# First loads reordered, the product with g split around the first scores, and one turn a step later in a chunked-attention-plus-MLP kernel

## The chip, the cores and the metric

The kernel runs on one core of a Trainium2 chip. The number that counts is device time in microseconds (us), and lower is better. Before the change the median of 7 runs is 225.18 us, the lowest 224.84 and the highest 226.16. Besides these there is one profiled execution, whose records are shown below.

## The reference

Two stages follow each other. The first is attention in chunks of 32 queries. Each chunk sees 16 keys to the left of it, its own 32, 8 to the right, and 8 memory keys. The second is a normalisation without bias, a product with `w_ch1`, a relu, a product with `w_ch2`, and a residual.

```python
# q, k, v: (4, 8, 768, 64); mem_k, mem_v: (4, 8, 8, 64)
for c in range(24):
    l, r = max(0, 32 * c - 16), min(768, 32 * c + 40)
    k_full = concat(mem_k, k[:, :, l:r]); v_full = concat(mem_v, v[:, :, l:r])
    a = softmax(q[:, :, 32 * c : 32 * c + 32] @ k_full.T / 8)
    attn[:, :, 32 * c : 32 * c + 32] = a @ v_full
x = attn with heads side by side                     # (4, 768, 512)
xn = (x - mean(x)) / sqrt(var(x) + 1e-6) * g_ln
out = x + relu(xn @ w_ch1) @ w_ch2                   # 512 -> 2048 -> 512
```

## The kernel before, in words

The tokens of the four batches are cut into 24 tiles of 128, six to a batch. Three tiles make a unit of 384 tokens, so there are eight units. The order of all work is written out by hand, because each engine executes its own list in order. A tile's attention consists of these steps:

- `scores(b, t)` (L303): 16 matmuls of keys against queries, 64 contraction rows each. They read the key windows `KT` and the queries `QR`, both with the head dimension on partitions.
- `soften` (L313): two exponentials on ScalarE.
- `values` (L324): 16 matmuls against `V`. Then VectorE divides by the sum of the exponentials (reciprocal L331, product L332) and forms the mean.
- `norm` (L344, VectorE): subtracts the mean and multiplies by `gb`, which is g spread over 128 partitions.
- `turn_x` (L372 and L377): transposes the normalised tile `xn` to `xT`. For tiles in `ON_PE` it uses four TensorE transposes and a VectorE copy; for others it uses a DMA transpose. `stats` and `root` form the standard deviation beside this, on ScalarE and GpSimd.

A unit's MLP is `up` (L398, 4 matmuls of 384 columns and a relu) sixteen times, then `down` (L424, 4 matmuls of 512 columns) twelve times. For unit 0 the first pieces are done tile by tile in `up_tile` (L409, 16 matmuls of 128 columns), because its tiles are finished one at a time.

Keys and queries must be turned so that the head dimension lies on partitions. A block of 256 tokens is rearranged by VectorE (`mix`, L104), turned by eight TensorE transposes (`transpose_block`, L218) and copied to the key windows (`window`, `pieces`) or to `QR` (`part_q`, `whole_q`). The first block of batch 0 comes in float32 over the queues of SyncE (SP) and ScalarE (ACT) into `raws`, and is narrowed by `mix_raw`. Its queries come in two halves of 64 partitions, lower and upper, with an even and an odd part each. `first_q` turns one half, and `first_copy` copies it to `QR`. All else is loaded by GpSimd (POOL), narrowing from float32 to float16 on the way: `load_block` (L120), `load_v` (L128), `load_w1` (L140) and `load_w2` (L145). GpSimd's list alternates loads with memsets, and at most eight loads are in flight, each on its own semaphore.

`mem_keys` turns the memory keys and `memT` copies them to `memKT`; `mem_cols` puts them into the last 8 columns of each window. `v_mem` copies memory values into the last 8 rows of `V`. `warm` (L462) issues matmuls of zeros, whose result nobody reads. PSUM slots come from rings: two `att` slots and four `mm` slots, taken in turn by `slot`.

After the opening (L552 to L629) a plan is followed: units 0 to 7 with 28 steps each. In steps 0 to 15 of a unit one `up` goes first, in steps 16 to 27 one `down` (unit 0 is already past most of its `up`s and begins at step 12). Then come the pieces that `at(u, step, fn, ...)` has put there. `attend(8, 12, 16, 1)` is the attention of the last tile of unit 2, which is done during unit 1; its `turn_x` is at step 19. Batch 1's first loads, `early` (memsets of its `V` and `KT` on GpSimd) and `mem_v_loads` are at steps 14 and 15 of unit 0.

Of the kernel before, what the change touches and what calls it, by code (L numbers as in the profile page):

```python
# [8 lines left out]
FP32 = mybir.dt.float32  # L9
# [6 lines left out]
def kernel(  # L16
# [32 lines left out]
    memkf = sb.tile([128, 2, 64], FP32, name="memkf")  # L49
    memk16 = sb.tile([128, 2, 64], FP16, name="memk16")  # L50
# [49 lines left out]
    def copy(eng, out, in_):  # L100
        if eng is nc.scalar:
            eng.copy(out=out, in_=in_)
        else:
            eng.tensor_copy(out=out, in_=in_)  # L104
# [45 lines left out]
    def mem_keys():  # L150
        p = slot("att")
        pv = as16(p[:, 0, :])
        for half in range(2):
            for par in range(2):
                nc.tensor.matmul(
                    out=pv[64 * par : 64 * par + 64, 128 * half : 128 * half + 128],
                    lhsT=memk16[:, half, :], rhs=identity,
                    is_transpose=True, start=True, stop=True, tile_position=(0, 64 * par),
                )
        mem_slot.append(pv)  # L160
# [3 lines left out]
    def memT():  # L164
        pv = mem_slot[0]
        for par in range(2):
            rows = slice(64 * par, 64 * par + 64)
            nc.vector.tensor_copy(
                out=memKT[rows, :, :, :].rearrange("p b j m -> p b (j m)"),
                in_=free(pv[rows, :], 32 * par, [[64, 4], [1, 32]]),  # L170
            )
# [88 lines left out]
    def first_q(half, pvs):  # L260

        i = pick(iv, ("b", 0, 0, 1))
        rows = slice(64 * half, 64 * half + 64)
        for r in range(8):
            pv, c = (pvs[r // 4], 128 * (r % 4)) if len(pvs) == 2 else (pvs[0], 128 * r)
            nc.tensor.matmul(
                out=pv[:, c + 64 * half : c + 64 * half + 64],
                lhsT=i[rows, 128 * r : 128 * r + 128], rhs=identity[rows, rows],
                is_transpose=True, start=True, stop=True, tile_position=(64 * half, 0),
            )  # L270

    def first_copy(half, pvs):

        n = 8 // len(pvs)
        for m, pv in enumerate(pvs):
            copy((dve, act)[m], free(QR[0], 512 * m + 64 * half, [[128, n], [1, 64]]),
                 free(pv, 64 * half, [[128, n], [1, 64]]))
# [188 lines left out]
    nc.scalar.dma_start(out=grow, in_=dram(moe_g_ln, 0, [[512, 1], [1, 512]]))  # L466
# [9 lines left out]
    nc.sync.dma_start(out=memkf, in_=dram(mem_k, 0, [[64, 128], [128 * 64, 2], [1, 64]]))  # L476
    first_load(1, 0, 0, 16, nc.sync)
    first_load(1, 1, 0, 16, nc.scalar)

    def load_mem_v(b, eng):  # L480
        eng.dma_start(
            out=xs[5 + b][96:W, :], in_=dram(mem_v, b * 4096, [[64, 8], [512, 8], [1, 64]])
        )

    load_mem_v(0, nc.sync)
    first_load(1, 0, 16, 32, nc.sync)
    first_load(1, 1, 16, 32, nc.scalar)
# [18 lines left out]
    def mem_vals(b):  # L506
        copy(act, memv16[96:W, b, :, 0:64], xs[5 + b][96:W, :].rearrange("p (h d) -> p h d", h=8))

    make_identity(nc, identity)
    load_block(0, 1, 0)  # L510
    nc.gpsimd.memset(V[0].bitcast(FP32)[0:32, 0, :, :], 0.0)
    ones(0, 0, 2, pool)
    nc.vector.memset(zero, 0.0)
# [34 lines left out]
    load_v(0, 11)  # L548
    load_w2(2)
# [4 lines left out]
    warm(4)  # L554
    p = slot("att")
    nc.tensor.matmul(out=p[:, 0, :], lhsT=gone, rhs=grow, start=True, stop=True)
    mix_raw(0, raws[0], 0, dve)
    mix_raw(0, raws[0], 1, act)
    copy(dve, memk16, memkf)
    copy(act, gb, p[:, 0, :])  # L560
    warm(1, 128)
    transpose_block(0, 0, 0, K0)
    mem_keys()
    warm(1, 512, mm[2])
    window(0, 0, K0, 0, dve)
    mix_raw(1, raws[1], 0, dve, 0, 64)
    mix_raw(1, raws[1], 1, act, 0, 64)
    first_q(0, Q0)
    memT()
    window(0, 0, K0, 1, act)  # L570
    mem_cols(0, dve)
    first_copy(0, Q0)
    warm(1, 512, p[:, 1, :])
    scores(0, 0)
    mem_vals(0)
# [3 lines left out]
    rest = [as16(att[0][:, 0, :])]  # L579
    first_q(1, rest)  # L580
    v_mem(0, 0, 2, dve)
    first_copy(1, rest)
    warm(1, 512, mm[2])
    mix(0, 1, 0, dve)
    values(0, 0)
# [7 lines left out]
    warm(2, 512, p[:, 1, :])  # L593
# [4 lines left out]
    turn_x(0, 0)  # L598
# [36 lines left out]
    def attend(i, s0, s1, u):  # L635

        b, t = divmod(i, NT)
        at(u, s0, scores, b, t)
        at(u, s0, soften, b, t, 0)
        at(u, s0 + 1, soften, b, t, 1)  # L640
        at(u, s1, values, b, t)
        at(u, s1 + 1, norm, b, t)
        at(u, s1 + (3 if i in ON_PE else 2), turn_x, b, t)
        at(u, s1 + 2, stats, b, t)
        if i < 6:
            at(1, i % 3, root, b, t)
        else:
            at(i // 3 - 1, (20, 22, 23)[i % 3], root, b, t)

    def early(b):  # L650
        ones(1, 0, NG, pool)
        nc.gpsimd.memset(V[1][0:32, 0, :, :], 0.0)
        nc.gpsimd.memset(V[1][64:96, NG - 1, :, :], 0.0)
        clear_keys(1, pool)

    def mem_v_loads(b):
        for i in range(1, B):
            load_mem_v(i, nc.gpsimd)
# [14 lines left out]
    for b in range(1, B):  # L673
        at(0, 22 + b, mem_vals, b)
# [12 lines left out]
    order[1:1] = [(mem_v_loads, ()), (early, ())] + [(root0, (t,)) for t in range(3)]  # L687
    for n, (fn, args) in enumerate(order):
        at(0, 14 + n // 2, fn, *((1,) + args))
# [101 lines left out]
```

## Time and profile before

| | |
|---|---|
| median of 7 runs (lowest, highest) | 225.18 us (224.84, 226.16) |
| the profiled execution's own time | 224.52 us |
| its span | 222.8 us |
| TensorE busy | 213.7 us (96%) |
| weight loads busy | 131.2 us (59%) |
| VectorE, ScalarE, GpSimd busy | 134.3, 103.9, 98.9 us |
| moved by DMA | 27.72 MB, 124 GB/s on average |

The span is the time from the first to the last instruction, and 1.7 us of the execution lie around it. Busy time is the union of an engine's instructions. A matmul's record includes the time until its result is through, so a TensorE row can be busy while matmuls issue slowly. In a timeline row the first number is the start, the second the duration, and the bracket at the end says how long the engine sat idle ahead of it and what ended that.

### The profile page before, as it was taken

How to read it: one execution, taken by the hardware profiler on the slowest of the kernel's cores; microseconds unless marked ns; L12 is line 12 of the kernel's file. 1: busy time of each engine (PE TensorE's matmuls, PEld its weight loads, DVE VectorE, ACT ScalarE, POOL GpSimd, SP SyncE). 2: the span in 40 equal slices, each digit the busy share in tenths (PEclk: the TensorE clock that was granted, in tenths of full speed). 3: DMA queues.
4: the chain of work that ended last, by engine and by line, in shares of the span. 5: the costliest groups of instructions: out<-in, count | busy, mean ns of one | idle time of the engine just before them, and what ended most of it. 6: DMA issues, size and time to landing. Idle time of an engine off the chain costs nothing.

```text
span 222.8 us, 4976 instructions
## 1 busy us (share of the span) xinstructions
PE 213.7 (96%) x1957; PEld 131.2 (59%) x1957; DVE 134.3 (60%) x330; ACT 103.9 (47%) x220; POOL 98.9 (44%) x172
## 2 busy tenths in 40 slices
PE   7789999999998999999999999999999999999994
PEld 1457986557664566546664567446654666456553
DVE  6675586687869658834675678716845367234221
ACT  3472558547783146733781067424851365103200
POOL 8667653899888896211923793300021011100000
PEclk9999999999999999999999999999999999999999
DMA  6999999799999999898995799494112201211012
GB/s 145 204 196 191 201 192 205 135 64 212 191 102 146 229 183 146 93 160 197 130 158 99 99 159 169 74 205 115 21 30 74 94 14 36 71 55 42 0 47 94
DMA packets 72225, 27.72 MB, mean 124 GB/s; under 512 B 60273, under 2 KB 68209, under 8 KB 72202
## 3 DMA queue, kind: packets, MB, share of 16 engines
q0 software_dynamic: 45728, 14.61, 61.8%
q1 hardware_dynamic: 26168, 12.28, 25.9%
q10 hardware_dynamic: 306, 0.53, 0.8%
q8 instruction: 15, 0.25, 0.5%
q14 instruction: 8, 0.07, 0.1%
HBM read 30.28 MB, written 6.29 MB: 164 GB/s over the span
## 4 chain that ended last, share of the span: by engine, by line
PE 70%; DMA 19%; POOL 6%; DVE 3%; issue 1%; DVEq 0%; POOLq 0%
PE mm L398 31%; PE mm L424 30%; DMA w2c<-in_moe_w_ch_dram 8%; DMA w1c<-in_moe_w_ch_dram 4%; PE att L303 4%; DMA V<-in_v_dram 3%; DMA st<-in_q_dram 3%; PE att L324 3%; PE mm L446 2%; POOL V L128 1%; POOL st L120 1%; POOL rstd L359 1%; DVE xs L332 1%; POOL veps L355 0%; DVE V L104 0%
## 5 line engine op out<-in xcount | busy, mean ns | idle before, releaser
L424 PE MATMUL mm<-w2c,rT 128*128 128x512 f16 x368 | 82.8, 379 | 0.0
L398 PE MATMUL mm<-xT,w1c 128*128 128x384 f16 x448 | 78.6, 327 | 0.2 <-DVE KT L104 0.2
L398 PEld LDWEIGHTS <-w1c 128*128 128x128 f16 x448 | 49.1, 114 | 22.4 <-issue 0.4
L424 PEld LDWEIGHTS <-rT 128*128 128x128 f16 x368 | 34.9, 98 | 39.7
L392 DVE TENSOR_SCALAR rT<-mm 128x384 f16<-128x384 f32 (+1 forms) x61 | 34.3, 567 | 25.3 <-PE mm L398 21.9
L390 ACT ACTIVATE rT<-mm 128x384 f16<-128x384 f32 (+1 forms) x63 | 31.4, 502 | 38.2 <-PE mm L398 20.9
L313 ACT ACTIVATE AT<-att,band 104x512 f16<-104x512 f32 x48 | 31.3, 685 | 28.3 <-PE att L303 28.3
L128 POOL DMA_DIRECT2D V<-in_v_dram x48 | 38.3, 810 | 4.1 <-DMA w1c<-in_moe_w_ch_dram 2.7
L433 DVE SCALAR_TENSOR_TENSOR osb<-mm,rstd,xs 128x512 f32<-128x512 f32 x23 | 17.2, 749 | 34.2 <-PE mm L424 29.6
L355 POOL TENSOR_SCALAR veps<-sq 128x1 f32<-128x1 f32 x24 | 7.3, 303 | 62.0 <-ACT junk L349 48.3
L349 ACT ACTIVATE junk<-xs,nmean 128x512 f16<-128x512 f32 x24 | 17.3, 722 | 15.0 <-DVE nmean L338 13.1
L344 DVE SCALAR_TENSOR_TENSOR xn<-xs,nmean,gb 128x512 f16<-128x512 f32 x24 | 17.9, 747 | 0.4
L332 DVE SCALAR_TENSOR_TENSOR xs<-att,rec 128x512 f32<-128x512 f32 x24 | 16.6, 692 | 0.8
L303 PE MATMUL att<-QR,KT 64*104 64x64 f16 x384 | 16.0, 235 | 0.1
L303 PEld LDWEIGHTS <-KT 64*104 64x104 f16 x384 | 12.7, 135 | 4.8 <-issue 2.5
L359 POOL TENSOR_TENSOR rstd<-veps,mhalf 128x1 f32<-128x1 f32 x24 | 14.4, 598 | 2.0
L120 POOL DMA_DIRECT2D st<-in_q_dram x22 | 12.7, 593 | 5.0 <-DMA w2c<-in_moe_w_ch_dram 2.0
L409 PE MATMUL mm<-xT,w1c 128*128 128x128 f16 x192 | 13.8, 235 | 0.5 <-DVE xT L377 0.5
L120 POOL DMA_DIRECT2D st<-in_k_dram x22 | 13.2, 620 | 2.0 <-DVE xT L377 1.6
L409 PEld LDWEIGHTS <-w1c 128*128 128x128 f16 x192 | 12.7, 119 | 1.1 <-issue 1.0
L324 PEld LDWEIGHTS <-AT 104*64 104x64 f16 x384 | 8.4, 114 | 8.1 <-issue 3.9
L331 DVE RECIPROCAL rec<-att 128x8 f32<-128x8 f32 x24 | 4.9, 206 | 13.3 <-PE att L324 12.9
(79 smaller groups left out, 148.1 us busy)
## 6 DMA issues: line engine op xcount, KB each, us to landing
out_dram<-osb SPq DMA_DIRECT2D x23, 256.0 KB, 2.2
V<-in_v_dram POOLq DMA_DIRECT2D x40, 96.0 KB, 5.7
st<-in_k_dram POOLq DMA_DIRECT2D x22, 128.0 KB, 5.6
st<-in_q_dram POOLq DMA_DIRECT2D x22, 128.0 KB, 6.8
w1c<-in_moe_w_ch_dram POOLq DMA_DIRECT2D x4, 512.0 KB, 9.7
w2c<-in_moe_w_ch_dram POOLq DMA_DIRECT2D x4, 512.0 KB, 8.8
V<-in_v_dram POOLq DMA_DIRECT2D x8, 80.0 KB, 5.4
xT<-xn SPq DMA_TRANSPOSE x17, 2.8
```

Of the source, the lines that this page charges most:

```text
L120: nc.gpsimd.dma_start(out=s[:, 512 * par : 512 * par + 512], in_=dram((k, q)[which], (b * H + 4 * par) * HS + blk * 256 * D, [[512, 32], [ ...
L128: nc.gpsimd.dma_start(out=V[b % 2][lo:hi, g, :, 0:64], in_=dram(v, b * H * HS + (64 * g - 16 + lo) * D, [[64, hi - lo], [HS, H], [1, 64]]),)
L303: nc.tensor.matmul(out=p[0:W, par, (4 * gg + j) * 64 : (4 * gg + j) * 64 + 64], lhsT=KT[b % 2][rows, 2 * t + gg, j, :], rhs=free(QR[b % 2] ...
L313: nc.scalar.activation(out=free(AT[t % 3], 32 * c, [[64, 16], [1, 32]]), in_=free(p, 4 * c, [[64, 16], [1, 4], [8, 8]], W), func=ACTF.Exp, ...
L332: nc.vector.scalar_tensor_tensor(out=x.rearrange("p (h d) -> p h d", h=8), in0=free(p, 0, [[128, 8], [1, 64]]), scalar=1.0, in1=free(r, 0, ...
L344: nc.vector.scalar_tensor_tensor(out=xn[i % 4], in0=xs[i % 9], scalar=nmean[t], in1=gb, op0=ALU.add, op1=ALU.mult,)
L349: nc.scalar.activation(out=junk, in_=xs[(NT * b + t) % 9], func=ACTF.Square, bias=nmean[t], scale=1.0, accum_out=sq[t],)
L390: nc.scalar.activation(out=o, in_=p, func=ACTF.Relu)
L392: nc.vector.tensor_scalar(out=o, in0=p, scalar1=0.0, scalar2=None, op0=ALU.max)
L398: nc.tensor.matmul(out=p, lhsT=free(w1c[c][:, dt, :], i, [[4, 128]]), rhs=xT[u % 2][:, dt, 128 * lo : 128 * (lo + n)], start=(dt == 0), st ...
L409: nc.tensor.matmul(out=p[:, 128 * k_ : 128 * k_ + 128], lhsT=free(w1c[c][:, dt, :], k_, [[4, 128]]), rhs=xT[u % 2][:, dt, 128 * i : 128 * ...
L424: nc.tensor.matmul(out=p, lhsT=rT[c][:, k_, 128 * i : 128 * i + 128], rhs=w2c[c][:, k_, :], start=(c == 0 and k_ == 0), stop=(c == 3 and k ...
```

## The change

It has these parts:

1. First loads. ScalarE issues only the odd half of the first keys, without the load of g ahead of it. SyncE issues the even keys, the lower even queries, the memory keys, g, batch 0's memory values, and both parts of the upper queries. GpSimd issues the lower odd queries, ahead of everything else that it does; its first `load_block` now comes after two memsets.
2. Memory keys are loaded as 32 rows of 512 instead of 2 x 128 rows of 64, and turned by 16 transposes of 32 columns instead of 4 of 128. They come after the lower queries.
3. The spread of g is done in two matmuls of 256 columns, one ahead of `scores(0, 0)` and one behind it, into `mm[3]`; it was one of 512 columns at the start.
4. Both halves of the first queries are turned into `Q0[0]` and copied by `part_q`; the lower one by ScalarE, the upper one by VectorE.
5. `warm`: seven at the start instead of four; the five others of the first tile are gone; one instead of two before `scores(0, 1)`.
6. `turn_x(0, 0)` goes ahead of `scores(0, 1)`.
7. Tile 8 (unit 2's last tile): `turn_x` at step 20 instead of step 19.
8. GpSimd's memsets for batch 1 stand ahead of `load_w2(2)` instead of in step 14 of unit 0, and two of them write float32 words. The memory values of batches 1 to 3 come in one narrowing load straight into `memv16`, behind four `load_v` of batch 1; they came in three loads with a ScalarE copy for each.

```diff
--- before.py
+++ after.py
@@ -46,8 +46,8 @@
 
     identity = sb.tile([128, 128], FP16, name="identity")
     zero = sb.tile([128, 512], FP16, name="zero")
-    memkf = sb.tile([128, 2, 64], FP32, name="memkf")
-    memk16 = sb.tile([128, 2, 64], FP16, name="memk16")
+    memkf = sb.tile([32, 512], FP32, name="memkf")
+    memk16 = sb.tile([32, 512], FP16, name="memk16")
     memv16 = sb.tile([W, B, H, VW], FP16, name="memv16")
     memKT = sb.tile([128, B, 4, 8], FP16, name="memKT")
     gb = sb.tile([128, 512], FP32, name="gb")
@@ -150,11 +150,11 @@
     def mem_keys():
         p = slot("att")
         pv = as16(p[:, 0, :])
-        for half in range(2):
+        for m in range(8):
             for par in range(2):
                 nc.tensor.matmul(
-                    out=pv[64 * par : 64 * par + 64, 128 * half : 128 * half + 128],
-                    lhsT=memk16[:, half, :], rhs=identity,
+                    out=pv[64 * par : 64 * par + 64, 32 * m : 32 * m + 32],
+                    lhsT=memk16[:, 64 * m : 64 * m + 64], rhs=identity[0:32, 0:32],
                     is_transpose=True, start=True, stop=True, tile_position=(0, 64 * par),
                 )
         mem_slot.append(pv)
@@ -166,8 +166,8 @@
         for par in range(2):
             rows = slice(64 * par, 64 * par + 64)
             nc.vector.tensor_copy(
-                out=memKT[rows, :, :, :].rearrange("p b j m -> p b (j m)"),
-                in_=free(pv[rows, :], 32 * par, [[64, 4], [1, 32]]),
+                out=memKT[rows, :, :, :],
+                in_=free(pv[rows, :], 4 * par, [[8, 4], [1, 4], [32, 8]]),
             )
 
     def mem_cols(b, eng):
@@ -257,24 +257,17 @@
             copy(eng, free(o, 128 * r0 + 64 * par, [[128, n], [1, 64]]),
                  free(srcs[par][lo:hi, :], 64 * r0, [[64, n], [1, 64]]))
 
-    def first_q(half, pvs):
+    def first_q(half):
 
         i = pick(iv, ("b", 0, 0, 1))
         rows = slice(64 * half, 64 * half + 64)
         for r in range(8):
-            pv, c = (pvs[r // 4], 128 * (r % 4)) if len(pvs) == 2 else (pvs[0], 128 * r)
+            c = 128 * r + 64 * half
             nc.tensor.matmul(
-                out=pv[:, c + 64 * half : c + 64 * half + 64],
+                out=Q0[0][:, c : c + 64],
                 lhsT=i[rows, 128 * r : 128 * r + 128], rhs=identity[rows, rows],
                 is_transpose=True, start=True, stop=True, tile_position=(64 * half, 0),
             )
-
-    def first_copy(half, pvs):
-
-        n = 8 // len(pvs)
-        for m, pv in enumerate(pvs):
-            copy((dve, act)[m], free(QR[0], 512 * m + 64 * half, [[128, n], [1, 64]]),
-                 free(pv, 64 * half, [[128, n], [1, 64]]))
 
     def mix(b, blk, which, eng):
         s, o = pick(st, ("b", b, blk, which)), pick(iv, ("b", b, blk, which))
@@ -463,7 +456,6 @@
 
 
     raws = ((osb[0], osb[1]), (osb[2], xs[4]))
-    nc.scalar.dma_start(out=grow, in_=dram(moe_g_ln, 0, [[512, 1], [1, 512]]))
 
     def first_load(which, par, lo, hi, eng):
         eng.dma_start(
@@ -473,18 +465,21 @@
 
     first_load(0, 0, 0, 32, nc.sync)
     first_load(0, 1, 0, 32, nc.scalar)
-    nc.sync.dma_start(out=memkf, in_=dram(mem_k, 0, [[64, 128], [128 * 64, 2], [1, 64]]))
     first_load(1, 0, 0, 16, nc.sync)
-    first_load(1, 1, 0, 16, nc.scalar)
-
-    def load_mem_v(b, eng):
-        eng.dma_start(
-            out=xs[5 + b][96:W, :], in_=dram(mem_v, b * 4096, [[64, 8], [512, 8], [1, 64]])
-        )
-
-    load_mem_v(0, nc.sync)
+    first_load(1, 1, 0, 16, nc.gpsimd)
+    nc.sync.dma_start(out=memkf, in_=dram(mem_k, 0, [[512, 32], [1, 512]]))
+    nc.sync.dma_start(out=grow, in_=dram(moe_g_ln, 0, [[512, 1], [1, 512]]))
+
+    nc.sync.dma_start(out=xs[5][96:W, :], in_=dram(mem_v, 0, [[64, 8], [512, 8], [1, 64]]))
+
+    def load_mem_v():
+        nc.gpsimd.dma_start(
+            out=memv16[96:W, 1:B, :, 0:64].rearrange("p b h d -> p (b h) d"),
+            in_=dram(mem_v, 4096, [[64, 8], [512, 24], [1, 64]]),
+        )
+
     first_load(1, 0, 16, 32, nc.sync)
-    first_load(1, 1, 16, 32, nc.scalar)
+    first_load(1, 1, 16, 32, nc.sync)
 
     PAIR = 1.0 / 128 + 15.0 / 2**20
 
@@ -503,13 +498,13 @@
     def count_v(i, c, g):
         copy(dve, V[i][:, g, :, 64:80], free(cnt[0:W, c : c + 1], 0, [[0, H], [0, 16]]))
 
-    def mem_vals(b):
-        copy(act, memv16[96:W, b, :, 0:64], xs[5 + b][96:W, :].rearrange("p (h d) -> p h d", h=8))
+    def mem_vals():
+        copy(act, memv16[96:W, 0, :, 0:64], xs[5][96:W, :].rearrange("p (h d) -> p h d", h=8))
 
     make_identity(nc, identity)
-    load_block(0, 1, 0)
     nc.gpsimd.memset(V[0].bitcast(FP32)[0:32, 0, :, :], 0.0)
     ones(0, 0, 2, pool)
+    load_block(0, 1, 0)
     nc.vector.memset(zero, 0.0)
     nc.vector.memset(gone, 1.0)
     clear_keys(0, dve)
@@ -546,42 +541,45 @@
     load_w2(1)
     load_v(0, 10)
     load_v(0, 11)
+    ones(1, 0, NG, pool)
+    nc.gpsimd.memset(V[1].bitcast(FP32)[0:32, 0, :, :], 0.0)
+    nc.gpsimd.memset(V[1].bitcast(FP32)[64:96, NG - 1, :, :], 0.0)
+    clear_keys(1, pool)
     load_w2(2)
     load_w2(3)
 
     K0 = [as16(mm[0]), as16(mm[1])]
     Q0 = [as16(mm[2]), as16(mm[3])]
-    warm(4)
-    p = slot("att")
-    nc.tensor.matmul(out=p[:, 0, :], lhsT=gone, rhs=grow, start=True, stop=True)
+    def spread_g(half):
+        cols = slice(256 * half, 256 * half + 256)
+        nc.tensor.matmul(out=mm[3][:, cols], lhsT=gone, rhs=grow[:, cols], start=True, stop=True)
+
+    warm(7)
     mix_raw(0, raws[0], 0, dve)
     mix_raw(0, raws[0], 1, act)
-    copy(dve, memk16, memkf)
-    copy(act, gb, p[:, 0, :])
-    warm(1, 128)
     transpose_block(0, 0, 0, K0)
-    mem_keys()
-    warm(1, 512, mm[2])
-    window(0, 0, K0, 0, dve)
     mix_raw(1, raws[1], 0, dve, 0, 64)
     mix_raw(1, raws[1], 1, act, 0, 64)
-    first_q(0, Q0)
+    copy(dve, memk16, memkf)
+    first_q(0)
+    mem_keys()
+    window(0, 0, K0, 0, dve)
+    window(0, 0, K0, 1, act)
+    part_q(0, 0, 0, Q0[0], act)
+    spread_g(0)
     memT()
-    window(0, 0, K0, 1, act)
     mem_cols(0, dve)
-    first_copy(0, Q0)
-    warm(1, 512, p[:, 1, :])
     scores(0, 0)
-    mem_vals(0)
+    mem_vals()
     soften(0, 0, 0)
     soften(0, 0, 1)
     mix_raw(1, raws[1], None, dve, 64, 128)
-    rest = [as16(att[0][:, 0, :])]
-    first_q(1, rest)
     v_mem(0, 0, 2, dve)
-    first_copy(1, rest)
-    warm(1, 512, mm[2])
     mix(0, 1, 0, dve)
+    spread_g(1)
+    first_q(1)
+    part_q(0, 0, 1, Q0[0], dve)
+    copy(act, gb, mm[3])
     values(0, 0)
     norm(0, 0)
     window(0, 0, K0, 2, act)
@@ -590,12 +588,12 @@
     window(0, 1, Q0, 0, act)
     window(0, 1, Q0, 1, act)
     key_right(0, 3, act)
-    warm(2, 512, p[:, 1, :])
+    turn_x(0, 0)
+    warm(1, 512, mm[1])
     scores(0, 1)
     soften(0, 1, 0)
     soften(0, 1, 1)
     v_mem(0, 2, 4, dve)
-    turn_x(0, 0)
     turn["mm"] = 3
     up_tile(0, 0, 0, act)
     values(0, 1)
@@ -640,22 +638,12 @@
         at(u, s0 + 1, soften, b, t, 1)
         at(u, s1, values, b, t)
         at(u, s1 + 1, norm, b, t)
-        at(u, s1 + (3 if i in ON_PE else 2), turn_x, b, t)
+        at(u, s1 + (2, 3, 4)[(i in ON_PE) + (i == 8)], turn_x, b, t)
         at(u, s1 + 2, stats, b, t)
         if i < 6:
             at(1, i % 3, root, b, t)
         else:
             at(i // 3 - 1, (20, 22, 23)[i % 3], root, b, t)
-
-    def early(b):
-        ones(1, 0, NG, pool)
-        nc.gpsimd.memset(V[1][0:32, 0, :, :], 0.0)
-        nc.gpsimd.memset(V[1][64:96, NG - 1, :, :], 0.0)
-        clear_keys(1, pool)
-
-    def mem_v_loads(b):
-        for i in range(1, B):
-            load_mem_v(i, nc.gpsimd)
 
     def root0(b, t):
         root(0, t)
@@ -670,8 +658,6 @@
     at(0, 18, count_v, 0, 1, NG - 1)
     attend(4, 17, 20, 0)
     attend(5, 19, 22, 0)
-    for b in range(1, B):
-        at(0, 22 + b, mem_vals, b)
 
     U = 28
 
@@ -684,9 +670,10 @@
     order = [(load_pair, (0,))] + [(load_v, (g,)) for g in range(4)]
     order += [(load_pair, (1,)), (mem_cols, (pool,)), (load_v, (4,)), (load_v, (5,))]
     order += [(load_pair, (2,))] + [(load_v, (g,)) for g in range(6, 12)]
-    order[1:1] = [(mem_v_loads, ()), (early, ())] + [(root0, (t,)) for t in range(3)]
+    order[1:1] = [(root0, (t,)) for t in range(3)]
+    order[8:8] = [(load_mem_v, None)]
     for n, (fn, args) in enumerate(order):
-        at(0, 14 + n // 2, fn, *((1,) + args))
+        at(0, 14 + n // 2, fn, *(() if args is None else (1,) + args))
     at(0, 20, count_v, 1, 0, 0)
     at(0, 20, count_v, 1, 1, NG - 1)
     at(0, 22, mix, 1, 0, 0, dve)
```

## The prediction

> **What bounds the kernel now.** I read the page first, then the table by stretches of time, then the waits of TensorE, then the timeline of the two places where TensorE is not full.
>
> ```profile
> span 222.8 us, 4976 instructions
> PE 213.7 (96%) x1957; PEld 131.2 (59%) x1957; DVE 134.3 (60%) x330; ACT 103.9 (47%) x220; POOL 98.9 (44%) x172
> ...
> PE   7789999999998999999999999999999999999994
> ...
> DMA  6999999799999999898995799494112201211012
> ...
> 65.00:70.00 5.00, 4.35 (x36) 1.87 (x34) 4.74 (x12) 2.04 (x5) 5.00 (x10) 1.00 0.87 107
> 80.00:90.00 10.00, 10.00 (x115) 6.96 (x113) 7.79 (x20) 6.95 (x15) 7.00 (x10) 1.00 2.17 159
> ```
>
> TensorE is the bound: from slice 4 on its digit is 9 almost everywhere, and 80 to 90 us has no idle time. Time can be won only where it is short of work: in the first 22 us, in 65 to 70 us, and in the tail, which the change leaves alone. The DMA digits of the first 15 slices show that the loads are close to saturated while the first tile waits for its own.
>
> ```profile
> 0.72 0.68 SPq L469 DMA_DIRECT2D osb<-in_k_dram  x1
> 1.44 1.33 POOL L120 DMA_DIRECT2D st<-in_k_dram  x2
> 5.81 1.03 PE L218 MATMUL mm<-identity,iv 128*128 128x128 f16 x8 [0.53 <-DVE iv L104]
> 8.53 0.29 DVE L104 CAST iv<-osb 64x256 f16<-64x256 f32 x1 [1.34 <-DMA osb<-in_q_dram]
> 9.08 0.61 PE L266 MATMUL mm<-identity,iv 64*128 64x64 f16 x8 [1.34 <-DVE iv L104]
> 10.16 0.90 PE L303 MATMUL att<-QR,KT 64*104 64x64 f16 x16
> 12.42 0.65 PE L324 MATMUL att<-V,AT 104*64 104x65 f16 x16 [0.38 <-ACT AT L313]
> 16.78 1.87 PE L409 MATMUL mm<-xT,w1c 128*128 128x128 f16 x16 [0.52 <-DVE xT L377]
> 19.56 1.91 PE L409 MATMUL mm<-xT,w1c 128*128 128x128 f16 x16
> 22.83 1.06 PE L409 MATMUL mm<-xT,w1c 128*128 128x128 f16 x16
> ```
>
> In the opening the lower queries land last (8.5), after the keys (turned at 5.81). The rest is a chain through the engines. The last two rows are the same 16 matmuls: 1.91 us at 19.56 and 1.06 at 22.83. TensorE runs at about half speed until some 22.4 us, though the table prints 1.00 for the clock.
>
> ```profile
> 60.11 0.81 PE L398 MATMUL mm<-xT,w1c 128*128 128x384 f16 x4 [0.18 <-DVE KT L104]
> 66.73 0.93 DVE L104 COPY V<-memv 8x2560 f16<-8x2560 f16 x1
> 69.19 0.75 DVE L344 SCALAR_TENSOR_TENSOR xn<-xs,nmean,gb 128x512 f16<-128x512 f32 x1
> 70.00 0.40 PE L372 MATMUL att<-identity,xn 128*128 128x128 f16 x4 [0.65 <-DVE xn L344]
> ```
>
> At 70.00 TensorE stood idle for 0.65 us until VectorE, busy 4.74 of 5 us, had finished tile 8's `xn`.
>
> **The change part by part, against the profile's own 222.8 us.**
>
> *First loads (part 1).* The odd keys were issued at 1.28 and landed at 5.15; without g ahead of them they are issued at 0.73. SP's even keys, issued at 0.72, took 3.2 us to land. Two transfers of 256 KB together: I take 4.3. ScalarE's table load stood at 3.25 behind four DMA issues; it now comes behind one, so ScalarE is ready. Keys turn at about 4.7 instead of 5.81. The lower even queries move from SP's third to its second issue (2.08 to 1.40). The odd ones become GpSimd's first instruction, at about 0.65. Their cost on that queue is not in the trace; the nearest row is GpSimd's first load (1.44), whose first half landed after 4.2 us. Later V loads there took 6.7 to 7.2. So they land between 4.9 and 7.8; I take 5.3, near the first row, with the queue as empty as it was then. That is 3.2 us earlier than 8.5. The Trainium skill speaks against this move: "DMA: Bandwidth & Descriptors", section "SWDGE vs HWDGE vs iDMA", says that GpSimd's descriptors are made by software and SP's and ACT's by hardware with a faster setup. The trace agrees: GpSimd's first packet came 2.7 us after its issue (4.13), SP's 1.5 us after (2.2). By the rule alone the half belongs on ACT, some 1.2 us quicker than on GpSimd with equal issue times; by the rows, ACT's issue of it stood at 1.95 and landed after 6.2 us, behind the keys. The rows decide: 5.3.
>
> *The chain to the first scores.* VectorE narrows the queries 5.3 to 5.9 (2 x 0.29), ScalarE to 6.1 (2 x 0.40). `first_q` follows to 6.75 (0.61), then the 16 key turns to about 7.3 (between 0.43 and 0.9 us; the four old ones took 0.42). The windows (0.73 on VectorE, 0.49 on ScalarE) and the query copy (0.55) run beside. `memT` (0.45) and `mem_cols` (0.26) end at 8.05. The first half of g (about 1.0 us, half of the old 2.07) ends at 8.2. Scores start at 8.2 instead of 10.16, and with two exponentials (1.26) `values` could go at 10.45 instead of 12.42.
>
> *What is late next.* V's first two groups landed at 10.5 and 10.8. The DMA engines are full from 2.5 us on, so earlier queries don't bring V earlier; GpSimd's list also starts about 0.7 us later (one more load ahead). I take 11.1 for `values`: 1.3 of the 2.0 us remain. Upper queries: SP alone now, landing at 9.3 (before 9.4 and 10.1), narrowed by 10.15, turned by 10.85. VectorE then has `v_mem` 0.49, `mix` 0.70 and the upper `part_q` 0.55, until 11.9. Behind these waits the reciprocal (13.14 before), so `xn` ends at 13.8 (15.05 before), and the turn of the next keys waits for `part_q` at 11.9 (before 13.0). Copying `gb` (0.58, ScalarE, after the exponentials) lies beside this.
>
> *Tile 0's turn ahead of the scores, fillers gone.* The turn goes at 13.8, `xT` is ready at 14.85, the last key edge at 14.1. One filler of 0.43, scores at 14.65 (14.82 before), and `up_tile` right behind them at 15.5 instead of 16.78. The removed fillers stood in gaps; they cost nothing and save nothing by themselves. Weights: w1's first quarter landed at 13.0, its second at 16.7 for a use at 19.56, later ones with 3 us to spare. So the opening is 1.28 us ahead.
>
> *What that is worth depends on the clock.* If full speed still comes at 22.4, work done earlier at half speed replaces work at full speed: 1.28 / 2, about 0.65. If it comes earlier, `values(0, 1)` at 17.35 and VectorE's 2.5 us to `xn` bound the next turn (21.1 instead of 22.36), so 1.3. "TensorE: Matmul & The Clock Gate", "Part 1", states that the switch needs one busy window of 3.4 us on a free-running grid. Here the last 3.4 us up to the switch have matmuls issuing 78% of the time, the ones before them 76%, with the 0.52 us wait at 16.78 in them. By the rule the new order, without a gap from 13.8 on, switches at 17.2 to 20.7; by the one row it stays at 22.4. I take the middle, 1.0 us.
>
> *Tile 8's turn (part 7).* It issues no DMA. TensorE goes on with the key turns (0.45; their `mix` ended at 68.1) and four `down` matmuls (0.86), so it gets to the turn at 70.7, and `xn` is ready at 69.95. The 0.65 us go. Behind it `xT` is needed by unit 2's `up` at its step 0, about 7 us later: covered. If VectorE were over 0.7 us later still, the wait would come back.
>
> *GpSimd's list (part 8).* Memsets of 2.1 us move from 39.5 to 28.4, where it waited 1.40 for a DMA; `load_w2(2)` slips by up to 0.7 us, and has 4.7 to spare (landed 38.6, used at 43.3). Two fewer load issues and ring waits: batch 1's loads go 3 to 5 us earlier, into the DMA slices with 5 and 7. The wait of VectorE at 57.2 for queries (0.77) and the 0.18 of TensorE at 60.11 behind it should go; I count 0.10. Three ScalarE copies fall away where ScalarE is no bound: nothing. VectorE may run slower beside GpSimd's memsets at 28 to 30 (a cast at 39.5 took 0.76 against 0.23 to 0.35 elsewhere); the next key turn has 1.7 us to spare.
>
> *Sum:* 1.0 + 0.65 + 0.10 = 1.75 us. The span becomes 221.05, the execution 222.8 (1.7 around it). The profiled one, 224.52, lies 0.66 below the median of 225.18, so the forecast for the median is 223.4.
>
> **Rivals.**
>
> *GpSimd's queue eats the opening (0.15).* From the landing of the lower queries to the scores there are 2.9 us in the new order against 1.65 in the old. With 7.3 instead of 5.3 the opening gains nothing; V slipping by 1.3 us does the same. For it: the 6.7 to 7.2 us rows. Against: these were issued behind full queues. Then only 0.65 + 0.10 remain: 224.4.
>
> *The clock switches later: slower (0.10).* Five fillers are gone, and TensorE idles from 13.0 to 13.8 for `xn`. If that costs a window, 3.4 us run at half speed: 1.7 us. With two, 3.4. It decides once the switch comes later than 22.4 + 2 x 1.4 = 25.2 us (0.65 + 0.75 are gained by then). One window gives 225.5, two give 227.2; I put the case at 226.2. Against it: no gap from 13.8 on.
>
> *Middle gain is hidden (0.13).* VectorE is nearly full at 65 to 70, so its lag may come out at a later instruction, and part 7 brings nothing: 1.0 remains, 224.2.
>
> **How the numbers follow.** The first case has the remaining 0.62, with 222.2 to 224.0 for its own spread (clock 0.65 or 1.3, or a whole window of 1.7 won). Low end 222.2. The rivals at 224.2 and 224.4 lie inside; the high end of 225.2 leaves out the slower case and some of the low side. Runs differ by up to 1.3 us, and their median by perhaps 0.3%, or 0.68 us; that is what a measurement can tell from no change. Faster needs under 224.5: 0.62 + 0.13 and about a third of 0.15, so 0.78, with what spread takes off. Same 0.12, slower 0.10.
>
> **What the profile after would show.** Right: scores of tile 0 near 8.2, `values` near 11.1 and waiting for V, `up_tile` near 15.5, no wait ahead of tile 8's turn, batch 1's V loads near 41. Wrong: ScalarE or VectorE waiting for odd queries past 7 us; 16 `up_tile` matmuls still at 1.9 us after 22.4; the 0.65 us wait turning up at another row between 65 and 75.

## The result and the profile after

The changed kernel takes 222.95 us in the median of 12 runs (222.49 to 223.56), beside 225.05 us for the kernel before on the same chip (31 runs). The ratio is 0.990, with a 95% interval of 0.988 to 0.992: 2.1 us faster. 223.4 was forecast. The sum came out nearly right, but two of its three terms did not: the opening, forecast at 1.0 us, is worth nothing that the runs can see, and GpSimd's list, forecast at 0.10 us, carries most of the gain. Ratios here and below leave slow executions out; there was one, of the kernel called open.

The profiled execution of the changed kernel took 223.56 us, with a span of 221.8. First the page, then the table by stretches of time.

```profile
span 221.8 us, 4995 instructions
PE 211.7 (95%) x1969; PEld 130.9 (59%) x1969; DVE 134.7 (61%) x329; ACT 102.2 (46%) x217; POOL 98.4 (44%) x171
...
PE   5778999999999999999999999999999999999993
...
DMA  6999999999989999177993799694112211210012
```

```profile
65.00:70.00 5.00, 5.00 (x45) 2.58 (x44) 4.76 (x13) 2.30 (x7) 4.44 (x9) 1.00 1.12 163
80.00:90.00 10.00, 10.00 (x115) 6.98 (x113) 8.49 (x21) 7.04 (x15) 3.98 (x8) 1.00 1.50 151
```

TensorE is now full from 65 to 70 us, where it had 4.35 of 5. A DMA slice with 7 became 9: the eighth, from 39.0 to 44.5 us, which batch 1's loads now fill. The slices with 5 and 7, into which the forecast put those loads, lie at 117 to 128 us and are still low, 3 and 7. The opening of the changed kernel in the timeline:

```profile
1.25 0.72 POOL L461 DMA_DIRECT2D xs<-in_q_dram  x1 [0.82 <-POOLq L762]
6.11 1.03 PE L218 MATMUL mm<-identity,iv 128*128 128x128 f16 x8 [1.77 <-DVE iv L104]
6.81 0.58 DVE L104 CAST iv<-osb 64x256 f16<-64x256 f32 x1 [0.76 <-DMA osb<-in_q_dram]
7.52 0.78 DVE L104 CAST memk<-memkf 32x512 f16<-32x512 f32 x1
10.04 0.90 PE L296 MATMUL att<-QR,KT 64*104 64x64 f16 x16
12.56 0.65 PE L317 MATMUL att<-V,AT 104*64 104x65 f16 x16
15.33 0.61 PE L365 MATMUL att<-identity,xn 128*128 128x128 f16 x4 [1.16 <-DVE xn L337]
17.13 1.90 PE L402 MATMUL mm<-xT,w1c 128*128 128x128 f16 x16
18.96 0.55 PE L317 MATMUL att<-V,AT 104*64 104x65 f16 x16
19.66 1.06 PE L402 MATMUL mm<-xT,w1c 128*128 128x128 f16 x16
21.55 0.40 PE L365 MATMUL att<-identity,xn 128*128 128x128 f16 x4 [0.83 <-DVE xn L337]
22.56 0.61 PE L218 MATMUL mm<-identity,iv 128*128 128x128 f16 x8 [0.61 <-ACT KT L102]
23.01 1.06 PE L402 MATMUL mm<-xT,w1c 128*128 128x128 f16 x16
```

The line numbers are those of the changed kernel: L296 is the scores, L317 the values, L365 the turn of `xn`, L402 `up_tile`. The queries are there at 6.8 instead of 8.5, but the first scores start at 10.04 against 10.16, the first `up_tile` at 17.13 against 16.78, and the third at 23.01 against 22.83. The opening is not ahead. Full speed of TensorE came earlier: the second `up_tile` takes 1.06 us here and took 1.91. But the 0.85 us saved there turn into waiting. TensorE now stands idle for 0.83 us ahead of tile 1's turn and for 0.61 us ahead of the key turns. In the kernel before, the rows of tile 1's values, of its turn and of the key turns were

```profile
18.58 0.65 PE L324 MATMUL att<-V,AT 104*64 104x65 f16 x16
21.34 0.61 PE L372 MATMUL att<-identity,xn 128*128 128x128 f16 x4
22.36 0.64 PE L218 MATMUL mm<-identity,iv 128*128 128x128 f16 x8 [0.40 <-ACT KT L102]
```

What holds them is VectorE's and ScalarE's chain behind tile 1's values. From these values to the key turns it takes 3.8 us before the change (18.58 to 22.36) and 3.6 us after it (18.96 to 22.56).

The middle of the changed kernel:

```profile
66.56 0.82 DVE L104 COPY V<-memv 8x2560 f16<-8x2560 f16 x1
68.92 0.75 DVE L337 SCALAR_TENSOR_TENSOR xn<-xs,nmean,gb 128x512 f16<-128x512 f32 x1
69.02 0.61 PE L218 MATMUL mm<-identity,iv 128*128 128x128 f16 x8
70.33 0.39 PE L365 MATMUL att<-identity,xn 128*128 128x128 f16 x4
```

VectorE is nearly as late with tile 8's `xn` as before (ready at 69.7, before at 69.9), but TensorE does the key turns and four `down` matmuls first and reaches the turn at 70.33, without a wait.

### The profile page after: what moved, and what is told of

Its sections match the earlier page's. It is cut to its first block, busy times and chain, and to the rows that moved or that the text cites. A ratio compares the mean times of both kernels' runs of the same rounds, so it can differ in the third digit from the quotient of the medians.

```text
span 221.8 us, 4995 instructions
## 1 busy us (share of the span) xinstructions
PE 211.7 (95%) x1969; PEld 130.9 (59%) x1969; DVE 134.7 (61%) x329; ACT 102.2 (46%) x217; POOL 98.4 (44%) x171
## 4 chain that ended last, share of the span: by engine, by line
PE 79%; DVE 0%; issue 0%; DVEq 0%
PE mm L417 34%; PE mm L391 34%; PE att L296 5%; PE att L317 3%; PE mm L439 2%; PE att L218 1%; PE mm L218 1%; PE att L365 0%; DVE osb L444 0%; DVEq L444 0%
## 5 line engine op out<-in xcount | busy, mean ns | idle before, releaser
L391 PEld LDWEIGHTS <-w1c 128*128 128x128 f16 x448 | 49.0, 114 | 22.0
L128 POOL DMA_DIRECT2D V<-in_v_dram x48 | 39.5, 837 | 6.0 <-DMA w1c<-in_moe_w_ch_dram 3.6
L348 POOL TENSOR_SCALAR veps<-sq 128x1 f32<-128x1 f32 x24 | 6.7, 278 | 66.8 <-ACT junk L342 53.3
L325 DVE SCALAR_TENSOR_TENSOR xs<-att,rec 128x512 f32<-128x512 f32 x24 | 16.6, 692 | 0.8
L296 PE MATMUL att<-QR,KT 64*104 64x64 f16 x384 | 16.0, 235 | 0.1
L296 PEld LDWEIGHTS <-KT 64*104 64x104 f16 x384 | 12.7, 135 | 4.7 <-issue 3.4
L120 POOL DMA_DIRECT2D st<-in_k_dram x22 | 13.7, 649 | 1.7 <-DVE V L104 1.7
L120 POOL DMA_DIRECT2D st<-in_q_dram x22 | 13.2, 629 | 1.4 <-DMA w2c<-in_moe_w_ch_dram 1.1
L402 PE MATMUL mm<-xT,w1c 128*128 128x128 f16 x192 | 12.9, 227 | 0.0
L317 PEld LDWEIGHTS <-AT 104*64 104x64 f16 x384 | 8.3, 113 | 7.3 <-issue 4.3
L402 PEld LDWEIGHTS <-w1c 128*128 128x128 f16 x192 | 11.9, 116 | 0.4
```

Source lines behind the costliest of these rows:

```text
L120: nc.gpsimd.dma_start(out=s[:, 512 * par : 512 * par + 512], in_=dram((k, q)[which], (b * H + 4 * par) * HS + blk * 256 * D, [[512, 32], [ ...
L128: nc.gpsimd.dma_start(out=V[b % 2][lo:hi, g, :, 0:64], in_=dram(v, b * H * HS + (64 * g - 16 + lo) * D, [[64, hi - lo], [HS, H], [1, 64]]),)
L296: nc.tensor.matmul(out=p[0:W, par, (4 * gg + j) * 64 : (4 * gg + j) * 64 + 64], lhsT=KT[b % 2][rows, 2 * t + gg, j, :], rhs=free(QR[b % 2] ...
L391: nc.tensor.matmul(out=p, lhsT=free(w1c[c][:, dt, :], i, [[4, 128]]), rhs=xT[u % 2][:, dt, 128 * lo : 128 * (lo + n)], start=(dt == 0), st ...
L402: nc.tensor.matmul(out=p[:, 128 * k_ : 128 * k_ + 128], lhsT=free(w1c[c][:, dt, :], k_, [[4, 128]]), rhs=xT[u % 2][:, dt, 128 * i : 128 * ...
```

## The experiments

All ratios are to the kernel before on the same chip, with 95% intervals. The last two columns split the span of each profiled execution at the start of the third `up_tile`: the start itself, and the rest of the span behind it. The rest is free of the opening's scatter. It is the printed span less the printed start, good to about 0.1 us, and each row has one profile.

| label | what it is | ratio (interval) | third `up_tile` at | span behind it |
|---|---|---|---|---|
| (before) | | 1 | 22.83 | 200.0 |
| (after) | changed | 0.9902 (0.9883 to 0.9921) | 23.01 | 198.8 |
| p7 | before + part 7 | 0.9970 (0.9951 to 0.9989) | 22.12 | 200.6 |
| p8 | before + part 8 | 0.9930 (0.9902 to 0.9957) | 23.12 | 199.6 |
| p78 | before + parts 7, 8 | 0.9918 (0.9894 to 0.9942) | 22.70 | 198.7 |
| open | changed, without 7 and 8 | 1.0037 (1.0012 to 1.0061) | 22.38 | 202.2 |
| after2 | changed, once more | 0.9919 (0.9896 to 0.9941) | 22.14 | 198.9 |
| p7m | p7 + part 8's memsets | 0.9882 (0.9838 to 0.9926) | 22.76 | 198.6 |
| p7v | p7 + part 8's memory values | 0.9904 (0.9867 to 0.9941) | 23.04 | 199.0 |
| act | changed, odd queries by ScalarE | 0.9907 (0.9873 to 0.9941) | 23.65 | 198.6 |
| fill | changed + 7 fillers | 0.9855 (0.9820 to 0.9891) | 21.40 | 198.9 |
| late_turn | changed, tile 0's turn behind the scores | 0.9869 (0.9839 to 0.9898) | 21.92 | 198.7 |
| opn2 | changed, g early, memory keys by ScalarE | 0.9926 (0.9895 to 0.9956) | 22.78 | 198.6 |
| best | fill and late_turn | 0.9851 (0.9817 to 0.9885) | 21.14 | 198.8 |

### Which part carries the gain: p7, p78, open, after2

p7 is one line in the kernel before; p78 adds part 8 of the diff to it, and open takes both back from the changed kernel.

```diff
-        at(u, s1 + (3 if i in ON_PE else 2), turn_x, b, t)
+        at(u, s1 + (2, 3, 4)[(i in ON_PE) + (i == 8)], turn_x, b, t)
```

> The kernel before with part 7 alone: tile 8's turn at step 20. If the 0.65 us wait ahead of that turn is a real loss of TensorE time, the run is 0.6 to 0.7 us faster (ratio 0.997) and no row between 65 and 75 us shows a wait. If VectorE's lag only comes out at another row, the ratio is 1.000.

> The kernel before with parts 7 and 8: tile 8's turn and GpSimd's shorter list, the opening untouched. The prediction's terms give 0.75 us (ratio 0.9967). The rival, that the middle holds most of the measured 2.1 us, gives 1.2 us or more (0.9947), since the two traces differ by 1.2 us between 23 and 87 us. VectorE's wait for queries at 57 us should be gone.

> The changed kernel with parts 7 and 8 taken back: the new opening alone. The prediction's term for it is 1.0 us (ratio 0.9956). The rival, read from the one profile after, where the first up_tile starts at 17.13 against 16.78, is that the opening wins no time before 17 us and is worth only what an earlier clock switch gives, between 0 and 1.7 us from run to run.

> The changed kernel once more beside the others on the same chip, for a second profile of its opening: ratio 0.990. If the opening is as in the first profile, first up_tile near 17.1 again; if that profile had a late landing of the keys by chance, some 1 us earlier.

Part 7 alone gave 0.3%, 0.68 us of 225.1, as forecast; the interval reaches from 0.25 to 1.1 us. Parts 7 and 8 in the old opening gave 0.82%, 1.85 us, the same as the changed kernel beside them (0.81%). So the new opening adds nothing to them; by an estimate from the two intervals (the root of the sum of their squares) it is worth no more than 0.75 us either way. Without them it made the kernel slower, by 0.37%. The two profiles of the changed kernel differ by 0.87 us at the third `up_tile`, nearly as much as the opening was to gain. Over all six profiles with the old opening that matmul group starts at 22.76 us on average, over the three with the new one as it stands (after, after2, open) at 22.51: 0.25 us earlier.

Where part 8 is missing, time is lost near 57 us, at the keys and queries of batch 1's second block of 256 tokens. From the timelines of the kernel before (the first three rows), of p7 (the next two) and of open (the last three):

```profile
54.76 0.43 DVE L104 COPY iv<-st 128x1024 f16<-128x1024 f16 x1 [0.21 <-DMA st<-in_k_dram]
56.32 0.61 PE L218 MATMUL mm<-identity,iv 128*128 128x128 f16 x8
57.20 0.43 DVE L104 COPY iv<-st 128x1024 f16<-128x1024 f16 x1 [0.77 <-DMA st<-in_q_dram]
```

```profile
56.25 0.43 DVE L104 COPY iv<-st 128x1024 f16<-128x1024 f16 x1 [2.53 <-DMA st<-in_k_dram]
56.74 0.45 PE L218 MATMUL mm<-identity,iv 128*128 128x128 f16 x5 [1.07 <-DVE iv L104]
```

```profile
56.88 0.43 DVE L104 COPY iv<-st 128x1024 f16<-128x1024 f16 x1 [2.90 <-DMA st<-in_k_dram]
57.36 0.62 PE L218 MATMUL mm<-identity,iv 128*128 128x128 f16 x8 [1.43 <-DVE iv L104]
60.46 0.81 PE L391 MATMUL mm<-xT,w1c 128*128 128x384 f16 x4 [0.67 <-DVE rec L324]
```

In p7 and open VectorE waits 2.5 and 2.9 us for the keys, and TensorE behind it 1.07 and 1.43 us for the rearranged keys; in open another 0.67 follows, behind VectorE's wait of 1.21 us for the queries. The waits of TensorE from 23 to 80 us that p7 has and p78 has not add up to 1.6 us, and their spans behind the third `up_tile` differ by 1.9. So most of the difference lies behind this block. The changed kernel's rows at that place have no bracket:

```profile
54.78 0.77 DVE L104 COPY iv<-st 128x1024 f16<-128x1024 f16 x1
...
56.53 0.61 PE L218 MATMUL mm<-identity,iv 128*128 128x128 f16 x8
56.55 0.42 DVE L104 COPY iv<-st 128x1024 f16<-128x1024 f16 x1
```

The reason is GpSimd's issue. The first two rows are the block's keys and queries in the kernel before, the next two those in the changed kernel:

```profile
48.37 1.15 POOL L120 DMA_DIRECT2D st<-in_k_dram  x2
49.47 1.13 POOL L120 DMA_DIRECT2D st<-in_q_dram  x2
```

```profile
44.38 1.15 POOL L120 DMA_DIRECT2D st<-in_k_dram  x2
45.49 1.11 POOL L120 DMA_DIRECT2D st<-in_q_dram  x2
```

The issue is 4.0 us earlier, and the four transfers also took less time to land, before the change

```profile
DMA to landing us min/median/max: 5.4/6.2/7.1
```

and after it

```profile
DMA to landing us min/median/max: 3.5/3.9/4.5
```

In the kernel before, the block was landed between 53.7 and 57.1, in p7 between 55.6 and 57.7, in open between 55.9 and 58.9, in the changed kernel between 47.9 and 50.5. Work that TensorE has finished sooner cannot help ahead of such a landing: with the old list, p7's profile was 0.71 us ahead at the third `up_tile`, and still the span behind it grew from 200.0 to 200.6. Two things met there. TensorE reached the key turns 0.65 us earlier than in the profile before (55.67, its wait taken off, against 56.32), and the keys landed 1.5 us later (56.23 against 54.73), though they were issued only 0.4 us later. With the landing of the profile before, p7 would not have waited for them; with p7's landing, the kernel before would have waited 0.42 us.

Why open is slower than the kernel before is settled only in part. Its block was issued 0.66 us later (49.03 against 48.37; its GpSimd list has one more load in front) and its four transfers landed 1.4 to 2.2 us later. How much of that is the extra load, and how much the scatter that p7 shows too, one profile can't tell.

### Which half of part 8: p8, p7m, p7v

p7m moves only part 8's memsets ahead of `load_w2(2)` (two of them then write float32 words); p7v replaces only the three loads of memory values and their ScalarE copies by one load behind four V loads.

```diff
 p7m:
+    ones(1, 0, NG, pool)
+    nc.gpsimd.memset(V[1].bitcast(FP32)[0:32, 0, :, :], 0.0)
...
     load_w2(2)
...
 p7v:
...
-    order[1:1] = [(mem_v_loads, ()), (early, ())] + [(root0, (t,)) for t in range(3)]
+    order[1:1] = [(early, ())] + [(root0, (t,)) for t in range(3)]
+    order[9:9] = [(load_mem_v, None)]
```

> The kernel before with part 8 alone. Parts 7 and 8 together gave 1.85 us, part 7 alone 0.68. If the two add up, part 8 alone gives 1.2 us (ratio 0.9948), and the trace still has a wait of some 0.6 us ahead of tile 8's turn near 69 us, but none at 55 to 60. The prediction's term for part 8 is 0.10 us (0.9996).

> Part 7, and of part 8 the memsets alone: they stand ahead of the load of w2's third quarter, the three loads of memory values stay as before. Theory (batch 1's second block of keys and queries lands too late, by up to 1.6 us, because GpSimd issues it late): its issue comes 2.5 to 2.8 us earlier, which is more than the wait, so nearly all of the gain is there, ratio 0.992 to 0.993. Rival (the gain of part 8 lies in ScalarE's three copies or in the ring waits of the three loads): ratio of part 7 alone, 0.997.

> Part 7, and of part 8 the memory values alone: one load behind four V loads instead of three ahead, without ScalarE's copies; the memsets stay where they were. Theory of the late second block: the three issues with their ring wait took from 36.0 to 39.4, so the block is issued about 2.5 us earlier, and the gain is nearly all there too, 0.992 to 0.993, though not the sum of the two. Rival that only the memsets count: 0.997.

Each half alone is enough. The block is issued at 45.3 in p7m and at 46.0 in p7v, and landed by 51.7 and 53.0, ahead of VectorE's first copies of it at 54.5 and 55.1. The spans behind the third `up_tile` are 198.6 and 199.0, against 198.7 with both halves and 200.6 with neither. In p7m ScalarE's copies and the three loads' ring waits are all still there, so the rival that the gain lies in them falls. It is one deadline, met or missed, and not a sum of saved work. p8 alone gave 0.7%, more than the 0.5% expected; there TensorE still waits for `xn` ahead of two turns, 0.5 us the longer time, as its waits from 23 to 80 us show (total, times, longest):

```profile
PE att L372 <- DVE xn L344: 0.9, 2, 0.5
```

Whether the gains of parts 7 and 8 add is not settled. Alone they are 0.3% and 0.7%, together 0.82% with an interval from 0.58 to 1.06%, so part 7 on top of part 8 is worth 0.12%, 0.3 us, with the noise larger than that.

### What holds the opening: act, fill, late_turn, opn2, best

The kernels act, fill, late_turn and opn2 start from the changed kernel. best has the first two edits of fill and the edit of late_turn.

```diff
 act:
-    first_load(1, 1, 0, 16, nc.gpsimd)
+    first_load(1, 1, 0, 16, nc.scalar)
 fill:
-    warm(7)
+    warm(11)
...
     transpose_block(0, 0, 0, K0)
+    warm(1)
...
+    warm(2, 512, mm[1])
     turn_x(0, 0)
 late_turn:
-    turn_x(0, 0)
-    warm(1, 512, mm[1])
+    warm(2, 512, mm[1])
     scores(0, 1)
...
+    turn_x(0, 0)
 opn2:
     first_load(0, 1, 0, 32, nc.scalar)
+    nc.scalar.dma_start(out=grow, in_=dram(moe_g_ln, 0, [[512, 1], [1, 512]]))
...
-    warm(7)
+    warm(5)
+    spread_g(0)
+    spread_g(1)
...
-    copy(dve, memk16, memkf)
+    copy(act, memk16, memkf)
```

In opn2 the load of g on SP and the two later calls of `spread_g` are gone, and `gb` is copied right behind the narrowing of the keys.

> The changed kernel with the odd part of the lower queries issued by ScalarE, behind its keys, instead of by GpSimd. The prediction by its rows: on ScalarE's queue they land later, 0.5 to 1 us slower than the changed kernel (ratio to before 0.993 to 0.995). By the skill's rule on who makes the descriptors: they land no later, and GpSimd's identity matrix and loads come 0.7 us earlier, ratio 0.989 to 0.991. Rival that nothing in the opening reaches the end: 0.992 as the changed kernel.

> The changed kernel with seven more fillers in TensorE's gaps: eleven at the start, one behind the first key turns, two ahead of tile 0's turn. They lie in idle time of the trace (1.95, 0.69 and 1.34 us). If the half clock is what the opening loses time to, full speed comes before 15 us, the first up_tile takes 1.06 us and not 1.9, and the run is about 1 us faster than the changed kernel (ratio to before 0.987). If VectorE's chain sets the opening, the clock comes earlier and the time stays, 0.991. If the fillers only delay the turns behind them, 0.993.

> The changed kernel with tile 0's turn behind the scores of tile 1 again, and two fillers ahead of these, as before the change. By the prediction the turn ahead of the scores wins part of the opening: 0.3 to 0.5 us slower than the changed kernel. By the traces TensorE stands 1.2 to 1.3 us idle for xn ahead of this turn, with the scores ready behind it, so the scores start about 1 us earlier and the first up_tile at most 0.5 us later or at the same time: no difference in the whole.

> The changed kernel with g loaded by ScalarE behind its keys and spread in TensorE's idle time before the first keys (5 fillers there instead of 7), gb copied ahead of the queries, and the memory keys narrowed by ScalarE instead of VectorE. If VectorE's list and the two halves of g hold up the chain behind the lower queries, the scores come 2.6 to 2.9 us after the queries' landing instead of 3.25, the upper queries' turn 1 us earlier, and the run is 0.4 to 1 us faster than the changed kernel (ratio to before 0.987 to 0.990). If the late landings alone set the opening: 0.991 to 0.992.

act: on ScalarE's queue the lower queries landed at 7.5 (odd) and 7.8 (even) instead of 6.2 and 6.8, and the scores started at 10.6. This is the order that the rows had given, against the rule on who makes the descriptors. The whole did not move by more than its interval.

opn2: the memory keys are off VectorE, and g is out of the chain, yet the scores start at 10.05, because `mem_cols` waits for the 16 turns of memory keys and the `memT` copies (1.09 us of TensorE waiting). The run is no faster. But the edit did not bring the memory keys forward: ScalarE had them narrowed at 8.30, as VectorE had in the changed kernel (7.52 and 0.78). So the two halves of g alone did not hold the scores; whether the memory keys do is left open.

fill: by the ratios the fillers brought 1.1 and 1.4 us over the two measurements of the changed kernel (0.9855 against 0.9902 and 0.9919; none of the two stood beside fill and late_turn, so that only the ratios to the kernel before can be compared). Its timeline:

```profile
5.92 0.62 PE L218 MATMUL mm<-identity,iv 128*128 128x128 f16 x8
9.05 0.90 PE L296 MATMUL att<-QR,KT 64*104 64x64 f16 x16 [0.41 <-ACT QR L102]
14.34 0.61 PE L365 MATMUL att<-identity,xn 128*128 128x128 f16 x4 [0.31 <-DVE xn L337]
16.03 1.08 PE L402 MATMUL mm<-xT,w1c 128*128 128x128 f16 x16
17.46 0.44 PE L317 MATMUL att<-V,AT 104*64 104x65 f16 x16 [0.35 <-ACT AT L306]
20.96 0.61 PE L218 MATMUL mm<-identity,iv 128*128 128x128 f16 x8 [0.61 <-ACT KT L102]
21.40 1.06 PE L402 MATMUL mm<-xT,w1c 128*128 128x128 f16 x16
```

The first key turns take 0.62 us where they took 1.03, and the first `up_tile` 1.08 where it took 1.90. The clock's record in the trace says the same: full from 5.5 to 8.9, half until 15.7, then full. These distances, 3.4 and 6.8 us, fit the grid of 3.4 us windows of the Trainium skill ("TensorE: Matmul & The Clock Gate", "Part 1"). That part of the forecast, that the opening's worth hangs on the clock, holds. The rows say how: the key turns come 3.5 us behind tile 1's values here too (17.46 to 20.96), so a faster clock pays when it comes ahead of these values, as here, and is waited away when it comes behind them, as in the changed kernel.

late_turn: faster than the changed kernel by 0.3 and 0.5% against its two measurements, 0.7 and 1.1 us, of which the first is within the noise. By the forecast it should have been 0.3 to 0.5 us slower.

```profile
14.97 0.90 PE L296 MATMUL att<-QR,KT 64*104 64x64 f16 x16
15.80 0.61 PE L365 MATMUL att<-identity,xn 128*128 128x128 f16 x4
16.93 1.05 PE L402 MATMUL mm<-xT,w1c 128*128 128x128 f16 x16 [0.52 <-DVE xT L370]
```

The scores start at 14.97 instead of 16.30 and 15.32 in the two profiles of the changed kernel, TensorE has no gap ahead of the turn, and the `up_tile` behind it already runs at full speed. The clock switched at 16.6 in this profile, at 19.2 and 18.7 in those two. How much of the gain is the place of the turn, and how much an early switch in this one profile, is not separated.

> Both that won: the fillers of the run with fillers (eleven at the start, one behind the first key turns) and tile 0's turn behind the scores of tile 1. If both act through an earlier full clock, they overlap: ratio to before 0.984 to 0.987, no better than the fillers alone (0.9855). If the turn's place wins by itself what TensorE stood idle for xn, they add up: 0.981 to 0.983.

best: 0.9851, 222.01 us, no faster than fill alone by more than the noise. The two changes overlap, as they should if both act by an earlier full clock: it switched at 15.8 here and at 15.7 in fill. Together with fill it has the lowest ratio of all, and both beat the changed kernel.

## Why the prediction was right in its sum and wrong in its terms

That the sum came out is luck. The opening was put 1.0 us too high and GpSimd's list 1.1 us too low, and the two errors cancel. Only the term of part 7 came out by itself.

- *Tile 8's turn: right.* 0.65 us forecast, 0.68 measured alone (p7), and the wait is gone without coming back between 65 and 75 us. On top of part 8 its worth is not resolved. VectorE's `xn` was ready 0.7 us ahead of the new place, as worked out.
- *GpSimd's list: the term that was mis-sized.* The step said that VectorE's 0.77 us at 57.2 and TensorE's 0.18 behind it should go, "I count 0.10". Part 8 is worth 1.2 us on top of part 7 and 1.6 alone. The step took the wait of one execution for its price. In p7's profile, with the same list, TensorE lost 1.07 us for the keys: it came 0.65 us earlier, and they landed 1.5 us later. Such a landing is a deadline that every gain ahead of it runs into, and one that lay 1.5 us apart in two profiles. The page of before had pointed at it, in the chain of waits, which I did not use:

```profile
PE 70%; DMA 19%; POOL 6%; DVE 3%; issue 1%; DVEq 0%; POOLq 0%
```

  Up to 57 us that chain runs through GpSimd's work and its loads, not through TensorE. In the first page of the changed kernel the line reads

```profile
PE 79%; DVE 0%; issue 0%; DVEq 0%
```

  and in its second, after2,

```profile
PE 76%; DMA 14%; POOL 6%; issue 2%; DVE 1%; DVEq 0%; POOLq 0%
```

  though no wait of TensorE behind 23 us ends with a load there. So the chain says where to look for a deadline, and not what it costs.

- *The offset of 0.66 us.* I carried the distance from the profiled execution to the median as a constant. The profile of before may be one in which that landing was early by chance (the V group ahead of the block landed at 52.1, in p7 at 55.0 and in open at 55.4), so that the usual execution waits longer. That would explain why part 8 is worth more than the waits in that profile. It is argued, not shown: there is one profile of the kernel before.
- *The opening: wrong.* Forecast at 1.0 us, it is worth nothing visible (p78 against after2). By the estimate above it is not worth more than 0.75 us. The steps that failed: keys at 4.3 (the halves landed at 4.2 and 5.4, while GpSimd's queue, which held the odd queries, was already moving data from 3.7 on), queries at 5.3 (6.8; SP's even half came last, GpSimd's odd half at 6.2 with an issue at 1.25 instead of 0.65), 2.9 us from there to the scores (3.25 and 2.6 in two profiles). V, named as what is late next, was not: it landed at 10.0, and `values` went at 12.56 behind the exponentials. So the signs named for the opening did not come (scores near 8.2, `values` near 11.1, `up_tile` near 15.5; in the profile 10.04, 12.56 and 17.13). Those named for the middle did: no wait ahead of tile 8's turn, and batch 1's V loads from 40.1 us on.
- *Tile 0's turn ahead of the scores: wrong in sign.* `xn` came at 15.3 and not at 13.8, and TensorE idled 1.16 us for it with the scores ready behind. late_turn, with the old order, was not slower but faster.
- *The clock: right in mechanism, worth less than taken.* It switched at 19.2 and 18.7 us, within the 17.2 to 20.7 of the forecast, and an earlier switch does shorten the opening (fill). But in the changed kernel it came behind the first `up_tile` and behind the start of tile 1's values. The forecast had named this bound, the values and VectorE's way from them to the next turn; it had the values at 17.35, and they came at 18.96 and 17.98 (18.58 before).
- *The rivals.* That GpSimd's queue eats the opening had the right effect by another cause, since GpSimd's half landed before SP's. That the clock switches later did not happen; of the fillers up to tile 1's scores eight stand where ten stood (four single ones are gone, not five, and a pair became one). That part 7 is hidden did not happen where it stands alone (p7).

## What to carry to other kernels

Ask of each load that ends a wait when it was issued and what sets that, and follow the chain of waits through queues before counting gains on the busy engine: what is gained ahead of such a landing is swallowed by it, as far as the landing does not come earlier too. Take its price from more than one profile, since the landing itself can scatter by more than the wait that one profile shows. Try alternatives with that deadline removed. And compare executions behind a common mark, such as the start of one matmul, when the opening scatters by more than the change is worth.

## What the runs showed of the hardware that I had not expected

- One V group on GpSimd's queue landed 3.5 us after the one ahead of it in p7 (51.5 and 55.0), while three output tiles were written by SP (issued from 47.8 on, landed by 55.4). By the packets of the trace GpSimd's queue moved 22 to 55 KB per half microsecond from 51.5 to 54 us, and 95 to 100 KB from 55 to 56 us, with the outputs through. In the changed kernel the block behind this V group landed by 50.5, so it stayed clear of that stretch; that this is why its transfers took 3.5 to 4.5 us and not 5.4 to 7.1 is likely, and no run separates it from the earlier issue.
- Full clock can come for one window and go again. after2 had it from 5.0 to 8.4 us with seven fillers, fill from 5.5 to 8.9 with eleven at the start, and open, the slowest of all, from 3.8 to 7.2. All three fell back to half, though TensorE's rows cover 3.10 of the next 3.41 us in after2 and 3.28 in fill.
- A window full of TensorE's rows was not enough for full clock. In the first profile of the changed kernel they cover all of 8.99 to 12.40 us, 3.41 us, and TensorE was still at half speed behind it: the key turns at 13.14 took 1.03 us, against 0.61 at 22.56. They cover all of 15.82 to 19.23 too, and at its end the clock switched. What tells the two apart no run here shows.
